# Attention and two gated layers on one core: VectorE's side work moves behind a pass's first sum

## The chip, the cores and the metric

The kernel runs on one core of a Trainium2 chip. The metric is the device time of one execution in microseconds (us). TensorE multiplies matrices into banks of PSUM; VectorE and ScalarE read those banks and do the elementwise work; GpSimd adds one operand per pass; SyncE's queue issues the transfers.

## What is computed

The reference is chunked attention, then two feed-forward layers (cut to what matters):

```python
x = attn_out.transpose(0, 2, 1, 3).reshape(3072, 512)
gate = 1.0 / (1.0 + np.exp(-(x @ w_gate)))      # 512 -> 1536
x = gate * (x @ w_val) @ w_out                  # 1536 -> 512
h = x @ w_in                                    # 512 -> 2048
out = h * (1.0 / (1.0 + np.exp(-h))) @ moe2_w_out   # 2048 -> 512
```

## The kernel before

Every float32 operand is split into a higher part, a rounded copy made on ScalarE (`nc.scalar.copy`, a CAST in the trace), and a lower part, what is left, made on VectorE by a subtraction (`split`, L90 to L99). A product of two operands is three matmuls of the parts: high by high, high by low, low by high.

The tokens stand in blocks. Layer one's first four blocks of 512 tokens are computed plainly, together with the attention of the blocks behind them. Its last 1024 tokens are the "new block" (`b = -1`), computed with seven products of sub-blocks in place of eight; layer two has three such blocks (`b` 0 to 2) of 1024 tokens. The work on one pair of output tiles is a pass (`pair2`): in the new block twelve passes, for six pairs a gate pass ("g") and a value pass ("v"), in a layer-two block eight passes ("l"). Behind the passes `out2` multiplies by the output weights.

A pass is seven products (`prod`) of six matmuls each into three banks: A11 into c1, S1 into c3, S2 into c2, A12 on top of c1, S3 on top of c2, S4 on top of c3, A22 on top of c2. Between two products on the same bank the bank has to be read:
- ScalarE copies c1 behind A11 (`s1`, L1066) and c3 behind S1 (`s5`, L1071); GpSimd adds `s1` to `s5`.
- the first sum `u2 = c2 + s1` is to be done on VectorE (`add`, L998) before S3 may go on with c2;
- the second sum `s5 = c2 + s5` before A22 may go on with c2;
- the third and the fourth sum, behind S4 and A22, bind no product of the same pass.

`done` puts sigmoid or silu (ScalarE) on the sums, `mult` multiplies a value by its gate (VectorE).

Every engine takes its instructions in the order in which the code emits them. Two kinds of side work are emitted among the products. The tail of a pass (`tail_of`): behind the second pass of a pair, the first difference of the output's operands (`sub`, L1001) and the split of the first operand (`form`). And the preparation of the output weights for layer two (`Pace`, `Pair2`): each weight tile is loaded, rebiased on ScalarE (L124), joined on VectorE (L134, L137), four differences are made (L633), the higher parts are cast on ScalarE (`coo`, L761), the lower parts made on VectorE (`lo_of`, L641), and both stored to DRAM (L731). `beat(n)` hands the preparation a time (`PREP2`, per kind of pass), and `Pace.go` emits steps until it is used up; stores are put out two beats behind. In layer one `PREP1` is the time handed out at each of three steps per tile. `prep.finish()` ahead of pass 6 of layer two's first block emits all that is left; then the preparation's pool of memory is closed, and the operands of the last pairs take its place. For `b` 1 and 2 there is no preparation.

Of the kernel before, what the change touches and what calls it, by code (L numbers as in the profile page):

```python
# [8 lines left out]
F32 = mybir.dt.float32  # L9
# [3 lines left out]
ALU = mybir.AluOpType  # L13
# [36 lines left out]
SLOT_C = {i: (n // 4, n % 4) for n, i in enumerate((A11, A12, S1, S2, S3, S4, A22))}  # L50
AHEAD2 = 4
DVE_US = {"meet": 2.1, "norm": 1.75}
PREP1 = 1.95
PREP2 = {"g": (0.4, 0.6, 1.1, 1.1), "v": (0.7, 0.7, 0.3, 0.3), "l": (0.9, 0.9, 1.1, 1.1)}


@with_exitstack
def moe_kernel(ctx: ExitStack, tc: tile.TileContext, qh, kh, vh, wg, wv, wo, w2i, w2o, out):
    nc = tc.nc
# [33 lines left out]
    def split(hi, lo, src, lo_eng, hi_eng=nc.scalar):  # L93

        if hi_eng is nc.scalar:
            nc.scalar.copy(hi, src)  # L96
        else:
            hi_eng.tensor_copy(hi, src)
        lo_eng.tensor_tensor(out=lo, in0=src, in1=hi.bitcast(F32), op=ALU.subtract)  # L99
# [11 lines left out]
    class Unit:  # L111
# [34 lines left out]
        def rest(self):  # L146
            nc.vector.tensor_tensor(
                out=self.u[:, 1], in0=self.t, in1=self.u[:, 0].bitcast(F32), op=ALU.subtract
            )
            if self.keep is not None:  # L150
                nc.sync.dma_start(out=self.keep, in_=self.u.bitcast(F32))
# [235 lines left out]
    with tc.manual_schedule():  # L387
# [169 lines left out]
        src = x32.pop(0)  # L557
# [386 lines left out]
        for b in range(-1, NB2):  # L944
            base[b] = len(granules)
            if b < 0:
# [4 lines left out]
                for i in ORDER2:  # L951
                    for q in range(NPAIRC // 2):
                        if i in (S1, S2, S3, S4):
                            outs.append(wco_d[(S1, S2, S3, S4).index(i), q])
                        else:
                            f, c = 4 * q + (i != A11), 256 * (i == A22)
# [8 lines left out]
        def next_granule():  # L965
            n = loaded[0]
            loaded[0] += 1
            if n >= len(granules):
                return
            w = w_slot(7 + n % NRING, f"wr{n}").rearrange("p a b c -> p (a b c)")  # L970
            k, src, *a = granules[n]
            if k == "o" or k == "m":
                w = w.rearrange("p (b a m c) -> p b a m c", b=2, a=2, m=2)
                if k == "o":
                    nc.sync.dma_start(out=w.bitcast(F32), in_=src)
                else:
                    for j, part in enumerate(src):
                        nc.sync.dma_start(out=w[:, j].bitcast(F32), in_=part)
            else:
                w = w.rearrange("p (a m c) -> p a m c", a=2, m=4)  # L980
                src = wc_d[src[0], src[1]] if k == "c" else w2i_d[src]
                nc.sync.dma_start(
                    out=w[:, :, : a[1]].bitcast(F32), in_=src[:, a[0], :, : a[1]]
                )
            ring[n] = w
# [4 lines left out]
        def bank(name):  # L990
            turn[0] += 1
            return (ps_m, ps_a, ps_m, ps_a, ps_y, ps_y, ps_y, ps_y)[(turn[0] - 1) % 8](name)

        def t2(name):
            return p2.tile([P, 512], F32, tag="t2", name=name, bufs=7)

        def add(o, a, b_):
            nc.vector.tensor_tensor(out=o, in0=a, in1=b_, op=ALU.add)  # L998
# [4 lines left out]
        def silu(o, i):  # L1003
            nc.scalar.activation(out=o, in_=i, func=AF.Silu)  # L1004
# [10 lines left out]
        def pair2(b, p, fill, tail, kind=""):  # L1015

            n = f"{b}_{p}{kind}"
            if kind:
                k = base[b] + 4 * p + 2 * "gv".index(kind)
            else:  # L1020
                k = base[b] + 2 * p
            slot = SLOT_C if kind else SLOT_L2
            final = [max(i, key=ORDER2.index) for i in ([j for j in slot if slot[j][0] == 0], [j for j in slot if slot[j][0]])]
            c1, c2, c3 = bank(f"c1_{n}"), bank(f"c2_{n}"), bank(f"c3_{n}")
            X = xp[b]

            def prod(o, i, first):
                half, m = slot[i]
                w = ring[k + half]
                j = 0  # L1030
                for kt in range(2):
                    for pw, px in ((0, 0), (0, 1), (1, 0)):
                        nc.tensor.matmul(  # L1033
                            o,
                            w[:, pw, m, kt * P : (kt + 1) * P],
                            X[i][:, px, kt],
                            start=first and j == 0,
                            stop=j == 5,
                            skip_group_check=not first,
                        )  # L1040
                        j += 1
                if i in final:
                    next_granule()

            def done(r, c):
                g = g2_of(b, p, r)
                if kind == "g":
                    nc.scalar.activation(out=g, in_=c, func=AF.Sigmoid)
                elif kind == "v":
                    wait.append((g, c))  # L1050
                else:
                    silu(g, c)

            def mult():
                while wait:
                    g, c = wait.pop(0)
                    nc.vector.tensor_tensor(out=g, in0=c, in1=g, op=ALU.mult)

            def beat(n):
                if b < 0 or b == 0 and p < NPAIR - 2:  # L1060
                    prep.go(PREP2[kind if kind else "l"][n] if p or kind == "v" or b == 0 else 0.0)

            wait = []
            s1, s5, u2 = t2(f"s1_{n}"), t2(f"s5_{n}"), t2(f"u2_{n}")
            prod(c1, A11, True)
            nc.scalar.copy(s1, c1)  # L1066
            if tail:
                tail()
            beat(0)
            prod(c3, S1, True)  # L1070
            nc.scalar.copy(s5, c3)  # L1071
            nc.gpsimd.tensor_tensor(out=s5, in0=s5, in1=s1, op=ALU.add)  # L1072
            if fill:
                fill()
            beat(1)
            prod(c2, S2, True)
            add(u2, c2, s1)
            prod(c1, A12, False)
            done("11", c1)
            prod(c2, S3, False)  # L1080
            add(s5, c2, s5)
            mult()
            done("22", s5)
            beat(2)
            prod(c3, S4, False)
            add(u2, c3, u2)
            mult()
            done("12", u2)
            prod(c2, A22, False)
            add(s1, c2, s1)  # L1090
            done("21", s1)
            mult()
            beat(3)

            def tail_of():
                pp = p // 2
                if p % 2 and kind != "g":

                    t = g2[b, pp, "12"]
                    sub(t, t, g2[b, pp, "11"])  # L1100
                    form(b, pp)

            return tail_of

# [12 lines left out]
                o, x, y = {S2: ("12", "22", "12"), S3: ("11", "12", "11"), A22: ("21", "21", "12")}[i]  # L1117
                sub(g2[b, pp, o], g2[b, pp, x], g2[b, pp, y])

        def form(b, m):  # L1120

            form_sum(b, m + 1)
            npp = npp_of(b)
            if m >= 7 * npp:
                return
            i, pp = ORDER2[m // npp], m % npp
            r = {A11: "11", S1: "12", S2: "12", A12: "21", S3: "11", S4: "22", A22: "21"}[i]
            src = g2[b, pp, r]
            f = p2.tile([P, 2, 2, 512], F32R, tag="gf", name=f"gf{b}_{m}", bufs=AHEAD2)
            split(f[:, 0], f[:, 1], src, nc.vector)  # L1130
            gf[b, m] = f

        def out2(b, beside):

# [83 lines left out]
        for bi, n in enumerate(BLOCKS1[:NB1]):  # L1218
# [3 lines left out]
            for f in range(NF1):  # L1222
                it = 3 * (bi * NF1 + f)

                def steps(i):
# [3 lines left out]
                    else:  # L1229
                        prep.go(PREP1 - sum(DVE_US.get(w, 0) for w, t in events.get(it + i, [])))  # L1230
                    if xgen is not None and (it + i) % 3 != 1:
# [53 lines left out]
        for b in range(-1, NB2):  # L1285
            tail = None
            if b < 0:
                for p in range(NPAIRC):
                    for kind in "gv":
                        fill = (lambda: emit_out1(*pending, t2)) if p + "gv".index(kind) == 0 else None  # L1290
                        tail = pair2(b, p, fill, tail, kind)
            else:
                for p in range(NPAIR):
                    if b == 0 and p == NPAIR - 2:
                        prep.finish()
                        pp_cm.__exit__(None, None, None)
                        p3_cm = tc.tile_pool(name="p3", bufs=1, side="right")
                        p3 = p3_cm.__enter__()
                    tail = pair2(b, p, None, tail)
            tail()  # L1300
            if b < 0:
                form(b, NPAIRC // 2)

            def beside(m):
                nonlocal xgen
                if b + 1 == NB2:
                    return
                if m == 0:
                    xgen = x_parts(b + 1, *load_y(b + 1))
                if m in ((4, 5, 6, 10, 11, 12, 17, 18, 19) if b < 0 else (4, 9, 10, 11, 16, 17, 24, 25, 26)):  # L1310
                    next(xgen, None)

            out2(b, beside)
# [76 lines left out]
```

## Time and profile before

| | |
|---|---|
| median of 3 runs | 1121.18 us (1121.1 to 1122.63) |
| profiled execution | 1124.1 us |
| its span | 1122.1 us, 2.0 us of the time lie around it |
| mean granted TensorE clock | 0.992 |
| TensorE, VectorE, ScalarE busy | 97%, 69%, 48% of the span |

The span runs from the first to the last instruction. The granted clock is a share of 2.4 GHz. A busy share is a mean over stages with different limits, and a wait on TensorE shows in the list of waits only if it leaves the engine idle; a slow clock does not show there.

### The profile page before, as it was taken

The page shows a single profiled execution, that of the slowest core. Times are in us where ns is not written, and L with a number is a line of the kernel's source. Part 1 is how long each engine was busy: PE and PEld are TensorE (multiplying, and loading weights), DVE is VectorE, ACT ScalarE, POOL GpSimd, SP SyncE. Part 2 cuts the span into 40 slices and gives each one's busy share as a digit, 9 for nine tenths or more (in the row PEclk, how much of TensorE's full clock was granted, in tenths as well). Part 3 has the DMA queues.
Part 4 walks back from the last instruction along what each step waited for, and adds up shares of the span by engine and source line. Part 5 has one row for each costly group of instructions (what it writes and reads, how often), then busy time and mean ns, then how long its engine had stood idle before and what let it go on. Part 6 is the DMA issues. An engine that isn't in the chain of part 4 may idle for free. (4 is left out here: it accounts for less than half of the span.)

```text
span 1122.1 us, 18930 instructions
## 1 busy us (share of the span) xinstructions
PE 1093.2 (97%) x7580; PEld 893.7 (80%) x7580; DVE 776.6 (69%) x1156; ACT 533.1 (48%) x791; POOL 65.6 (6%) x50
## 2 busy tenths in 40 slices
PE   7999999999999999999999998999999999999998
PEld 4888888888887788877778876788888888888887
DVE  7988787777777777567669857567833479443665
ACT  6766554364444453433434554354434455344442
POOL 0000000000000000011111001101011110011000
PEclk9999999999999999999999998999999999999999
DMA  8788688789877887687888697774755766655561
GB/s 317 274 282 298 230 299 298 274 294 316 310 256 266 288 323 260 227 284 262 295 293 329 196 337 256 271 301 169 251 195 192 269 231 228 207 197 206 195 217 76
DMA packets 106247, 288.02 MB, mean 257 GB/s; under 512 B 8624, under 2 KB 39344, under 8 KB 95408
## 3 DMA queue, kind: packets, MB, share of 16 engines
q1 hardware_dynamic: 105872, 286.43, 72.8%
q8 instruction: 60, 0.98, 0.4%
q10 hardware_dynamic: 288, 0.39, 0.1%
q14 instruction: 27, 0.22, 0.1%
HBM read 210.24 MB, written 76.55 MB: 256 GB/s over the span
## 5 line engine op out<-in xcount | busy, mean ns | idle before, releaser
L1033 PE MATMUL c<-xp,wr 128*128 128x512 f32 x1008 | 235.9, 397 | 8.4 <-DVE u L998 8.4
L1033 PEld LDWEIGHTS c<-xp,wr 128*128 128x128 f32 x1008 | 193.2, 192 | 50.6 <-DVE u L998 9.6
L1182 PE MATMUL o<-gf,wr 128*128 128x512 f32 x1008 | 229.0, 389 | 0.0
L1182 PEld LDWEIGHTS o<-gf,wr 128*128 128x128 f32 x1008 | 189.2, 188 | 39.3
L359 PE MATMUL pv<-x,w 128*128 128x512 f32 x564 | 138.5, 394 | 0.1
L359 PE MATMUL pg<-x,w 128*128 128x512 f32 x564 | 138.4, 394 | 0.1
L99 DVE TENSOR_TENSOR gf<-g,gf 128x1024 fp32r<-128x1024 f32 x84 | 103.9, 1239 | 49.7 <-ACT gf L96 49.2
L96 ACT CAST gf<-g 128x1024 fp32r<-128x1024 f32 x84 | 88.1, 1052 | 86.8 <-PE o L1182 71.5
L359 PEld LDWEIGHTS pv<-x,w 128*128 128x128 f32 x564 | 104.2, 188 | 23.2 <-DVE sg L374 0.4
L359 PEld LDWEIGHTS pg<-x,w 128*128 128x128 f32 x564 | 104.4, 188 | 22.1 <-DVE x L99 0.7
L376 ACT CAST g<-sg 128x512 fp32r<-128x512 f32 x48 | 29.8, 621 | 129.8 <-DVE sg L374 129.7
L998 DVE TENSOR_TENSOR s<-c,s 128x512 f32<-128x512 f32 x48 | 33.2, 691 | 66.3 <-PE c L1033 63.5
L1004 ACT ACTIVATE g<-s 128x512 f32<-128x512 f32 x48 | 30.3, 632 | 62.5 <-DVE s L998 62.5
L1001 DVE TENSOR_TENSOR g<-g,g 128x1024 f32<-128x1024 f32 x48 | 58.4, 1216 | 0.0
L1072 POOL TENSOR_TENSOR s<-s,s 128x512 f32<-128x512 f32 x24 | 35.4, 1476 | 335.7 <-ACT s L1071 335.7
L379 DVE TENSOR_TENSOR g<-sg,g 128x512 fp32r<-128x512 f32 x48 | 33.2, 691 | 26.1 <-ACT g L376 26.1
L998 DVE TENSOR_TENSOR u<-c,s 128x512 f32<-128x512 f32 x24 | 16.5, 688 | 40.2 <-PE c L1033 38.4
L369 ACT ACTIVATE sg<-pg 128x512 f32<-128x512 f32 x48 | 28.6, 596 | 31.2 <-PE pg L359 22.8
L108 PE MATMUL y<-g,wor 128*128 128x512 f32 x144 | 38.6, 390 | 0.0
L104 PE MATMUL y<-g,wor 128*128 128x512 f32 x144 | 38.5, 389 | 0.0
L106 PE MATMUL y<-g,wor 128*128 128x512 f32 x144 | 38.5, 389 | 0.0
L317 DVE STREAM_TRANSPOSE x<-sx 128x512 f32<-128x512 f32 x20 | 14.3, 716 | 33.8 <-PE sx L220 30.3
(596 smaller groups left out, 1574.0 us busy)
## 6 DMA issues: line engine op xcount, KB each, us to landing
wr<-w2o_d SPq DMA_DIRECT2D x42, 1024.0 KB, 4.8
wr<-w2i_d SPq DMA_DIRECT2D x24, 1024.0 KB, 5.5
wor<-wo_d SPq DMA_DIRECT2D x36, 512.0 KB, 7.1
wr<-w2i_d SPq DMA_DIRECT2D x24, 768.0 KB, 4.4
w2o_d<-coo SPq DMA_DIRECT2D x56, 256.0 KB, 6.9
w2i_d<-coi SPq DMA_DIRECT2D x24, 512.0 KB, 7.3
wr<-wc_d SPq DMA_DIRECT2D x12, 1024.0 KB, 6.3
v<-in_vh_dram SPq DMA_DIRECT2D x21, 512.0 KB, 5.6
```

The costliest lines, as they stand in the source:

```text
L96: nc.scalar.copy(hi, src)
L99: lo_eng.tensor_tensor(out=lo, in0=src, in1=hi.bitcast(F32), op=ALU.subtract)
L104: nc.tensor.matmul(o, w_hi, x_hi, start=first, stop=False)
L106: nc.tensor.matmul(o, w_hi, x_lo, start=False, stop=False)
L108: nc.tensor.matmul(o, w_lo, x_hi, start=False, stop=last)
L359: nc.tensor.matmul(o[:, :n], w[:, pw, kt * P : (kt + 1) * P], x[kt][:, px, :n], start=i == 0, stop=i == len(steps) - 1,)
L379: nc.vector.tensor_tensor(out=g[:, 1, :n], in0=sg[:, :n], in1=g[:, 0, :n].bitcast(F32), op=ALU.subtract)
L998: nc.vector.tensor_tensor(out=o, in0=a, in1=b_, op=ALU.add)
L1001: nc.vector.tensor_tensor(out=o, in0=a, in1=b_, op=ALU.subtract)
L1033: nc.tensor.matmul(o, w[:, pw, m, kt * P : (kt + 1) * P], X[i][:, px, kt], start=first and j == 0, stop=j == 5, skip_group_check=not first,)
L1072: nc.gpsimd.tensor_tensor(out=s5, in0=s5, in1=s1, op=ALU.add)
L1182: nc.tensor.matmul(c[at[i], dp], w[:, pw, pl, dp * P : (dp + 1) * P], f[:, px, pl], start=i in (A11, S1, S2) and pp == 0 and j == 0, stop= ...
```

## The change

In `pair2` the tail and the first beat, which stood behind the copy `s1`, are emitted behind the first sum, for the new block and layer two's first block; for `b` 1 and 2 the tail stays where it was. The beat behind S1 is gone, so a pass has three beats, with new times. `form` can return the lower part of its split as a function, which the pass calls behind the second sum. `PREP1` falls from 1.95 to 1.88.

```diff
-PREP1 = 1.95
-PREP2 = {"g": (0.4, 0.6, 1.1, 1.1), "v": (0.7, 0.7, 0.3, 0.3), "l": (0.9, 0.9, 1.1, 1.1)}
+PREP1 = 1.88
+PREP2 = {"g": (0.9, 1.5, 1.3), "v": (0.9, 0.7, 0.2), "l": (1.0, 1.8, 1.6)}
...
-            wait = []
+            wait, early = [], b > 0
             s1, s5, u2 = t2(f"s1_{n}"), t2(f"s5_{n}"), t2(f"u2_{n}")
+            rest = None
             prod(c1, A11, True)
             nc.scalar.copy(s1, c1)
-            if tail:
-                tail()
-            beat(0)
+            if tail and early:
+                tail()()
             prod(c3, S1, True)
             nc.scalar.copy(s5, c3)
             nc.gpsimd.tensor_tensor(out=s5, in0=s5, in1=s1, op=ALU.add)
             if fill:
                 fill()
-            beat(1)
             prod(c2, S2, True)
             add(u2, c2, s1)
+            if tail and not early:
+                rest = tail()
+            beat(0)
             prod(c1, A12, False)
             done("11", c1)
             prod(c2, S3, False)
             add(s5, c2, s5)
+            if rest:
+                rest()
             mult()
             done("22", s5)
-            beat(2)
+            beat(1)
...
-            split(f[:, 0], f[:, 1], src, nc.vector)
+            nc.scalar.copy(f[:, 0], src)
             gf[b, m] = f
+
+            def low():
+                nc.vector.tensor_tensor(
+                    out=f[:, 1], in0=src, in1=f[:, 0].bitcast(F32), op=ALU.subtract
+                )
+
+            if later:
+                return low
+            low()
```

On VectorE, at the start of pass 2 of layer two's first block (names `u_0_2`: block 0, pass 2; `u` is the first sum, `s` the second, `coo` lower parts, `gf` the lower split, `g` the difference), the order before was:

```order
L1001 TENSOR_TENSOR g_0_12_6892<-g_0_12_6892,g_0_11_6865 128x1024
L99 TENSOR_TENSOR gf_0_7009<-g_0_11_6865,gf_0_7009 128x1024
L641 TENSOR_TENSOR coo_0_6991<-fo_6927,coo_0_6991 128x512
L641 TENSOR_TENSOR coo_1_6993<-fo_6927,coo_1_6993 128x512
L641 TENSOR_TENSOR coo_2_7012<-fo_6927,coo_2_7012 128x512
L641 TENSOR_TENSOR coo_3_7015<-fo_6927,coo_3_7015 128x256
L998 TENSOR_TENSOR u_0_2_7000<-c_0_2_6996,s_0_2_6998 128x512
L998 TENSOR_TENSOR s_0_2_6999<-c_0_2_6996,s_0_2_6999 128x512
```

and is now, up to the third sum:

```order
L998 TENSOR_TENSOR u_0_2_7000<-c_0_2_6996,s_0_2_6998 128x512
L1001 TENSOR_TENSOR g_0_12_6897<-g_0_12_6897,g_0_11_6871 128x1024
L641 TENSOR_TENSOR coo_0_6973<-fo_6912,coo_0_6973 128x512
L641 TENSOR_TENSOR coo_1_6993<-fo_6912,coo_1_6993 128x512
L641 TENSOR_TENSOR coo_2_7026<-fo_6912,coo_2_7026 128x512
L641 TENSOR_TENSOR coo_3_7029<-fo_6912,coo_3_7029 128x256
L998 TENSOR_TENSOR s_0_2_6999<-c_0_2_6996,s_0_2_6999 128x512
L1139 TENSOR_TENSOR gf_0_7024<-g_0_11_6871,gf_0_7024 128x1024
L134 TENSOR_SCALAR stg_w2o_6952<-stg_w2o_6952 128x512
L137 SCALAR_TENSOR_TENSOR fo_7056<-stg_w2o_6952 128x2x256
L134 TENSOR_SCALAR stg_w2o_6954<-stg_w2o_6954 128x512
L137 SCALAR_TENSOR_TENSOR fo_7056<-stg_w2o_6954 128x512
```

The difference and the four lower parts moved from ahead of the first sum to between the first and the second, the lower split behind the second, ahead of two joins.

On ScalarE, from the end of pass 4 to the start of pass 6 of the same block (`s` copies of c1 and c3, `g` silu), the order before was:

```order
L761 CAST coo_0_7260<-fo_7205 128x512
L761 CAST coo_1_7262<-fo_7205 128x512
L1066 COPY s_0_5_7267<-c_0_5_7264 128x512
L761 CAST coo_2_7277<-fo_7205 128x512
L761 CAST coo_3_7280<-fo_7205 128x256
L1071 COPY s_0_5_7268<-c_0_5_7266 128x512
L1004 ACTIVATE g_2_11_7223<-c_0_5_7264 128x512
L1004 ACTIVATE g_2_22_7234<-s_0_5_7268 128x512
L1004 ACTIVATE g_2_12_7247<-u_0_5_7269 128x512
L1004 ACTIVATE g_2_21_7258<-s_0_5_7267 128x512
L1066 COPY s_0_6_7349<-c_0_6_7346 128x512
```

and is now:

```order
L1067 COPY s_0_5_7263<-c_0_5_7260 128x512
L1071 COPY s_0_5_7264<-c_0_5_7262 128x512
L1004 ACTIVATE g_2_11_7210<-c_0_5_7260 128x512
L1004 ACTIVATE g_2_22_7222<-s_0_5_7264 128x512
L1004 ACTIVATE g_2_12_7236<-u_0_5_7265 128x512
L1004 ACTIVATE g_2_21_7247<-s_0_5_7263 128x512
L761 CAST coo_0_7323<-fo_7224 128x512
L761 CAST coo_1_7325<-fo_7224 128x512
L761 CAST coo_2_7327<-fo_7224 128x512
L761 CAST coo_3_7330<-fo_7224 128x256
L1067 COPY s_0_6_7349<-c_0_6_7346 128x512
```

The last four casts moved from the start of pass 5 to its end, between its last silu and the first copy of pass 6.

On SyncE's queue the last stores (`w2o_d<-coo`) and the loads of weights (`wr`) stood, around the end of pass 5:

```order
L982 DMA wr_7312<-w2i_d 128x2x768
L731 DMA w2o_d<-coo_0_7260 128x2x256 x2
L731 DMA w2o_d<-coo_1_7262 128x2x256 x2
L975 DMA wr_7335<-w2o_d 128x2048
L731 DMA w2o_d<-coo_2_7277 128x2x256 x2
L731 DMA w2o_d<-coo_3_7280 128x2x256
```

and stand now:

```order
L982 DMA wr_7301<-w2i_d 128x2x768
L975 DMA wr_7319<-w2o_d 128x2048
L731 DMA w2o_d<-coo_0_7323 128x2x256 x2
L731 DMA w2o_d<-coo_1_7325 128x2x256 x2
L731 DMA w2o_d<-coo_2_7327 128x2x256 x2
L731 DMA w2o_d<-coo_3_7330 128x2x256
```

All seven stores stand behind the load that TensorE's last product of pass 5 releases.

## Rows read from the trace of the kernel before

**Rows 1.** The page, busy time of the engines.
```profile
PE 1093.2 (97%) x7580; PEld 893.7 (80%) x7580; DVE 776.6 (69%) x1156; ACT 533.1 (48%) x791; POOL 65.6 (6%) x50
```

**Rows 2.** The waits of TensorE: us in total, times, longest.
```profile
PE c L1033 <- DVE u L998: 8.4, 3, 3.5
...
PE c_-1_2g L1033 <- DVE u_-1_2g L998: 2.5, 1, 2.5
PE c_-1_4g L1033 <- DVE u_-1_4g L998: 2.4, 1, 2.4
...
PE c_-1_4v L1033 <- DVE u_-1_4v L998: 0.9, 1, 0.9
PE c_-1_0v L1033 <- DVE u_-1_0v L998: 0.8, 1, 0.8
```

**Rows 3.** The timeline of TensorE: start us, us, line, idle time before.
```profile
462.21 1.52 PE L1033 MATMUL c_-1_0g<-xp-1_0_5222,wr 128*128 128x512 f32 x6
...
537.13 1.52 PE L1033 MATMUL c_-1_3v<-xp-1_0_5222,wr 128*128 128x512 f32 x6
...
545.29 1.52 PE L1033 MATMUL c_-1_3v<-xp-1_5_5430,wr 128*128 128x512 f32 x6
...
550.73 1.52 PE L1033 MATMUL c_-1_4g<-xp-1_4_5389,wr 128*128 128x512 f32 x6
...
558.86 1.52 PE L1033 MATMUL c_-1_4v<-xp-1_0_5222,wr 128*128 128x512 f32 x6
...
588.61 1.52 PE L1182 MATMUL o_-1_0_6418<-gf-1_0_5788,wr 128*128 128x512 f32 x6
...
645.82 15.12 PE L1033 MATMUL c<-xp,wr 128*128 128x512 f32 x66
```

**Rows 4.** Windows: us, TensorE busy, granted clock, DMA share, GB/s.
```profile
514.00:516.00 2.00, 2.00 (x7) 0.50 1.00 403
...
556.00:558.00 2.00, 2.00 (x11) 1.00 0.96 353
...
680.00:682.00 2.00, 2.00 (x7) 0.50 0.18 11
```

**Rows 5.** The chain that ended last: start us, us, what.
```profile
813.60 76.16 PE c L1033 x336
```

**Rows 6.** The timeline of VectorE.
```profile
495.49 2.32 DVE L641 TENSOR_TENSOR coo<-fo,coo 128x512 fp32r<-128x512 f32 x4
...
507.10 1.22 DVE L1001 TENSOR_TENSOR g-1_0_12_5533<-g-1_0_12_5533,g-1_0_11_5515 128x1024 f32<-128x1024 f32 x1
508.23 2.31 DVE L99 TENSOR_TENSOR gf-1_0_5788<-g-1_0_11_5515,gf-1_0_5788 128x1024 fp32r<-128x1024 f32 x1
...
511.52 0.68 DVE L998 TENSOR_TENSOR u_-1_2g<-c_-1_2g,s_-1_2g 128x512 f32<-128x512 f32 x1
...
544.20 0.69 DVE L998 TENSOR_TENSOR s_-1_3v<-c_-1_3v,s_-1_3v 128x512 f32<-128x512 f32 x1 [2.03 <-PE c_-1_3v L1033]
...
559.67 0.42 DVE L134 TENSOR_SCALAR stg_w2o<-stg_w2o 128x512 int32<-128x512 int32 x1
...
562.06 2.65 DVE L633 TENSOR_TENSOR fo<-fo 128x256 f32<-128x256 f32 x4
...
721.39 1.23 DVE L99 TENSOR_TENSOR gf<-g,gf 128x1024 fp32r<-128x1024 f32 x1 [1.16 <-ACT gf L96]
```

**Rows 7.** The timeline of ScalarE in passes 6 and 7 of layer two's first block.
```profile
729.03 0.60 ACT L1004 ACTIVATE g<-c 128x512 f32<-128x512 f32 x1 [7.18 <-DMA w2o_d<-coo]
...
731.09 0.58 ACT L1066 COPY s<-c 128x512 f32<-128x512 f32 x1
```

**Rows 8.** The timeline of SyncE's queue, the last stores.
```profile
719.96 1.97 SPq L731 DMA_DIRECT2D w2o_d<-coo  x3
```

**Rows 9.** The line of the stores, L731, 56 of them.
```profile
DMA to landing us min/median/max: 4.8/6.9/8.2
```

**Rows 10.** The timeline of TensorE in layer one.
```profile
367.73 0.86 PE L308 MATMUL sx<-v,at 64*32 64x64 f32 x64 [2.33 <-ACT at L293]
```

More of the change, by code (lines that the diff above doesn't have):

```diff
@@ L1092, in pair2 @@
             mult()
-            beat(3)
+            beat(2)
             def tail_of():
@@ L1100, in tail_of @@
                     sub(t, t, g2[b, pp, "11"])
-                    form(b, pp)
+                    return form(b, pp, True)
+                return lambda: None
             return tail_of
@@ L1118, in form_sum, with form @@
                 sub(g2[b, pp, o], g2[b, pp, x], g2[b, pp, y])
-        def form(b, m):
+        def form(b, m, later=False):
             form_sum(b, m + 1)
@@ L1299, in moe_kernel @@
                     tail = pair2(b, p, None, tail)
-            tail()
+            tail()()
             if b < 0:
```

## The prediction

> **What bounds the kernel now.** The head of the profile's page comes first: TensorE is busy for 97% of the span, so only its waits and its slow stretches can be won; VectorE is busy for 69% [rows 1]. The list of what TensorE waited for comes next [rows 2]. One reason stands out: the products' line L1033 waits for a `u` made by VectorE at L998, in three waits of layer two's first block (8.4 us, the longest 3.5) and in four of the new block (2.5, 2.4, 0.9 and 0.8), 15.0 us in all. That `u` is the first sum of a pass, which reads bank c2 before the product S3 may add to it.
>
> A wait costs more than its length. From 537.13 to 545.29 stand six products, so one takes 1.36 us and a pass of seven 9.52 [rows 3]. From 550.73 to 558.86 four products took 8.13 us instead of 5.44: the 2.40 us wait in them cost 2.69, that is 0.29 for starting again, and the granted clock stayed at 1.00 behind it. Behind others it stood at 0.50 (1.2 GHz): behind the 2.45 us wait of the new block and the 3.5 us one of layer two [rows 4].
>
> The loss by stage: from 462.21 to 588.61 stand 516 matmuls (twelve passes of 42, twelve of layer one's). At the pace of a block without waits (336 in 76.16 us [rows 5]) they need 117.0 us and took 126.4: 9.4 lost. Layer two's first block began at 645.82 and ended, one such 76.16 before 813.60, at 737.44: 91.6 us for the same work, 15.3 lost besides the last matmul's own length [rows 3, 5]. Together 24.7 us. Of these 15.0 are the waits, 2.0 seven restarts at 0.29; the 7.7 left are slow clock. With four slow stretches, which I count in the windows, that is 1.9 us for one.
>
> **The change part by part.** T is the start of a pass on TensorE. In a pass without waits (537.13) the second sum starts at T+7.07, and A22, which needs it, at T+8.16 [rows 3, 6]. The first sum starts as long behind its product as the second (0.27), so at T+4.35, and must end before S3 at T+5.44.
>
> *Work moved from ahead of the first sum to behind it.* In the old order the subtraction, the lower split (2.31 us at 508.23) and a join stand ahead of it: the queue is busy from 507.10 to 511.52, where the sum starts without idle time; it ends at 512.2, and S3 had waited 2.45 us for it [rows 2, 6]. In the new order no beat and no tail of the pass itself stands there in any of the eighteen passes with such work, and what the pass before leaves there ends by T+4.6 where I added it up. All seven waits go: -24.7 us.
>
> *What now stands between the first and the second sum.* VectorE starts an instruction some 0.08 before the one ahead ends (508.23 behind the 1.22 us at 507.10), so a sum of 0.69 takes 0.61 of the queue, and there is room from T+4.96 to 8.16 - 0.69 - 0.04, T+7.43: 2.47 us. In most passes what stands there fits (the subtraction's 1.13 with one join, half of the 2.39 from 559.67 to 562.06). In passes 2 and 4 of layer two's first block it doesn't: the subtraction and all four lower parts (2.32, 2.25 to the next start) make 3.38 us [rows 6]. The second sum starts at T+8.34, 0.91 late, and with the restart costs 1.2, twice: +2.4. The low end is the bare 0.9 each, the high end a slow stretch more each.
>
> *What follows behind the second sum.* In those passes the lower split (1.23), two joins (2.39) and the third and fourth sum end at T+13.8; ScalarE's last silu (0.6) follows, and behind it in ScalarE's queue the next pass's copy of c1 (0.58 [rows 7]), which A12 waits for. It ends near T+15.0, where A12 is due at T+14.5 (its pass starts at 9.52 + 0.91): 0.5 late, with the restart 0.8, twice: +1.5. In the new block the gate passes of pairs 2 and 3 leave two casts between that silu and the copy, by the same sum 0.4 and 0.2 late: with restarts +1.2. The low end of these four is nothing, since a few tenths decide.
>
> In the value pass of pair 2 GpSimd's addition, late with that copy, meets VectorE's lower parts. Beside GpSimd a lower split took 2.31 us, and 1.23 elsewhere [rows 6], so 1.08 more; the second sum is then some 0.15 past its room, which I leave inside the range. The Trainium skill, "SBUF — State Buffer", section "SBUF: two separate sides", says that VectorE and GpSimd take a shared pair of ports as an exclusive lock, so that the later one waits for the whole of the other. The row agrees in kind; by the Trainium skill's rule, with GpSimd's whole addition in the way, the same place would cost about 0.3 instead of 0.15 us.
>
> *The last stores.* What is left of the preparation is finished at once behind pass 5: four casts, four lower parts and seven stores together, where before two lower parts and four stores went ahead during pass 5. The silu of pass 6 waits in ScalarE's queue for the last store, as its output lies in memory that the stores' pool gives back: 7.18 us, until 729.03 [rows 7]. Pass 6 began two passes before 737.44, at 718.40, so this is T+10.6; three more silus follow, and pass 7's copy of c1 starts at 731.09 and ends at T+13.27, where A12 needs it at T+13.56: 0.3 us to spare, so it shows as no wait. Now the casts can start only behind pass 5's last silu, at T+1.3, the last lower part (0.65 each) ends at T+4.4, and the stores, at 0.66 us each (three in 1.97), are issued up to T+6.6 instead of T+3.5 [rows 8]. With the median landing of 6.9 us [rows 9] the last lands near T+13.2; ScalarE goes on at T+13.4, the copy ends at T+16.1, 2.6 us late. Landings of 4.8 to 8.2 make this 0.5 to 3.9. Of the six waits of 2 us and over (the sixth is layer one's, at 1.00), four were followed by a slow stretch, so I take one: 2.6 + 0.3 + 1.9 = +4.8.
>
> *Layer one.* The smaller number for its beats shifts the preparation among the forward steps. Its one long wait, 2.33 us at 367.73, is for a copy behind a late gate product [rows 10]; in the new order two joins less stand ahead of the splits at that block's start, which should bring all behind them forward by 2.4 us. Another wait may open elsewhere, as the order changes over the whole layer. I take -1.0, with -2.6 and +2.4 as the ends.
>
> **The sum.** -24.7 + 2.4 + 1.5 + 1.2 + 4.8 - 1.0 = -15.8 us. The profiled execution's 1124.1 becomes 1108.3; the median, 2.9 below it at 1121.2, becomes 1105. A measurement of this kernel can tell about 0.2%, 2.2 us.
>
> **The rivals.** First, *the waits simply go*: the new waits stay at their low ends (0.9 twice, 0.5) and layer one gives its 2.6: -24.7 + 2.3 - 2.6 = -25, 1096 us. For it: all new waits but the two of 0.91 lie within a few tenths of their limits or hang on a landing time. Against it: those two are plain sums of rows. Chance 0.13.
>
> Second, *the waits move*: every larger new wait is followed by a slow stretch and the stores land late. Passes 2 and 4 cost 6.2, the last stores 6.1, the small ones 2.7, layer one 2.4: -24.7 + 17.4 = -7, 1114 us. For it: the 0.50 behind waits as short as 2.45 [rows 4]. Against it: all seven short and long waits of before made only four such stretches. Chance 0.10.
>
> Third, *slower*: the second sum becomes what the first was. Its room is 2.47 us in each of eighteen passes; if VectorE reaches it late in all of them, by 1.1 us and a restart on the mean, the 24.7 us are given back, and from there it is slower: 1124 us and more. For it: the same work must be done in the same passes. Against it: by the order sixteen of the eighteen have less than 2.47 us there, so that nearly every one would have to be stretched by an us, as 2.31 for 1.23 was, and VectorE has a third of the span free [rows 1]. Chance 0.03.
>
> Fourth, *no change*: the first sum isn't late for its queue but for its own input. The wait list names it seven times, and at 511.52 it starts with no idle time ahead of it [rows 2, 6]. Chance 0.02.
>
> **How the numbers follow.** The forecast has 0.72 and ends at about 1098 and 1111. The first rival lies around 1096; a range from 1097 to 1111 takes in a part of it and leaves out about 0.07 below and 0.13 above. Faster by over 0.2% is all but the last two rivals, 0.95; the same 0.02, slower 0.03.
>
> **What would show it.** In the list of waits L1033 no longer waits for the first sum, and waits about 0.9 us for the second sum in passes 2 and 4 of layer two's first block, some tenths for ScalarE's copy L1067 in the passes behind, and 2 to 3 us for that copy in the last pass, behind a silu that the last store releases. The windows show 1.00 everywhere but there. The forecast is wrong if the clock falls behind waits under one us, if the last stores land within 5 us, or if layer one shows a new wait.

## The result and the profile after

| | before | after |
|---|---|---|
| median, its runs | 1121.91 us (1121.1 to 1123.99, 4) | 1107.91 us (1106.93 to 1109.23, 4) |
| ratio | | 0.9873, interval 0.9855 to 0.9891 |
| profiled execution, its span | 1124.1, 1122.1 | 1109.23, 1107.1 |
| mean granted clock | 0.992 | 0.998 |

The kernel is faster by 1.27%, 14.0 us; 1105 was forecast, with 1097 to 1111 around it. The profiled executions differ by 14.9 us.

The list of TensorE's waits after, which answers to [rows 2]:

```profile
PE sx L220 <- issue: 1.7, 1, 1.7
PE c L1033 <- DVE s L998: 1.4, 2, 0.8
...
PE c L1033 <- ACT s L1067: 1.3, 1, 1.3
PE c_-1_5v L1033 <- DVE u_-1_5v L998: 1.2, 1, 1.2
...
PE pv L359 <- DVE sg L374: 0.8, 1, 0.8
PE c_-1_0g L1033 <- DMA wr<-wc_d: 0.6, 1, 0.6
```

The `u` of layer two's first block, 8.4 us before, is gone, and so are those of passes 2g, 4g, 4v and 0v of the new block. Three kinds stand in its place: 1.4 us for the second sum `s` in two passes, 1.3 for ScalarE's copy in one, and 1.2 for a first sum that had been in time, that of the value pass of pair 5 (5v). Layer one shows new waits too: the pause of 1.7 us that stands first in the list, 0.8 for `sg` and 0.6 for the first weights `wr`.

The timeline of TensorE after, which answers to [rows 3], shows the stages:

```profile
386.50 0.32 PE L220 MATMUL sx<-k,q 64*32 64x64 f32 x9 [1.75 <-issue]
386.75 4.61 PE L359 MATMUL pv<-x,w 128*128 128x512 f32 x12
...
465.11 1.63 PE L1033 MATMUL c_-1_0g<-xp-1_0_5194,wr 128*128 128x512 f32 x6 [0.56 <-DMA wr<-wc_d]
...
580.57 1.65 PE L1033 MATMUL c_-1_5v<-xp-1_3_5371,wr 128*128 128x512 f32 x6 [1.25 <-DVE u_-1_5v L998]
...
584.80 1.52 PE L1196 MATMUL o_-1_0_6425<-gf-1_0_5803,wr 128*128 128x512 f32 x6
...
641.92 8.32 PE L1033 MATMUL c<-xp,wr 128*128 128x512 f32 x36
...
716.76 5.73 PE L1033 MATMUL c<-xp,wr 128*128 128x512 f32 x24 [1.27 <-ACT s L1067]
722.33 1.98 PE L1196 MATMUL o<-gf,wr 128*128 128x512 f32 x8
```

The new block's passes take 119.7 us (465.11 to 584.80) where they took 126.4; at full pace they need 117.0. Layer two's first block takes 80.4 (641.92 to 722.33) where, first start to first start, it took 91.5; at full pace 76.2. So the passes gave back 17.8 us, and 7.0 of loss is left in them. But the new block starts at 465.11, not at 462.21 [rows 3]: layer one lost 2.9. The rest of the kernel is the same to 0.1 us.

The windows of TensorE after (us, busy, granted clock, DMA share, GB/s), which answer to [rows 4]:

```profile
388.00:390.00 2.00, 2.00 (x6) 0.50 1.06 413
580.00:582.00 2.00, 1.43 (x6) 1.00 1.06 406
670.00:672.00 2.00, 1.94 (x8) 1.00 0.80 312
718.00:720.00 2.00, 2.00 (x10) 1.00 0.07 29
```

No wait of the passes is followed by a slow stretch (a time at a granted clock of 0.50, 1.2 GHz) any more. The only one of the execution stands in layer one, behind the pause of 1.75 us at 386.50, for which the profile names no releaser.

### The profile page after: what moved, and what is told of

Same layout as the page of the kernel before. It is cut to its first block, busy times and chain, and to the rows that moved or that the text cites. A ratio compares the mean times of both kernels' runs of the same rounds, so it can differ in the third digit from the quotient of the medians.

```text
span 1107.1 us, 18923 instructions
## 1 busy us (share of the span) xinstructions
PE 1087.8 (98%) x7580; PEld 889.8 (80%) x7580; DVE 771.4 (70%) x1156; ACT 532.5 (48%) x791; POOL 64.2 (6%) x50
## 4 chain that ended last, share of the span: by engine, by line
PE 85%; DVE 7%; ACT 3%; DMA 3%; issue 1%; SPq 0%; DVEq 0%; ACTq 0%
PE o L1196 21%; PE c L1033 18%; PE pv L359 10%; PE pg L359 9%; PE y L108 3%; PE y L104 3%; PE y L106 3%; PE sx L308 1%; PE sx L220 1%; PE o_-1_1_6430 L1196 1%; PE o_-1_0_6429 L1196 1%; PE c_-1_0g L1033 1%; PE c_-1_4v L1033 1%; PE c_-1_5g L1033 1%; PE c_-1_1v L1033 1%
## 5 line engine op out<-in xcount | busy, mean ns | idle before, releaser
L1033 PE MATMUL c<-xp,wr 128*128 128x512 f32 x1008 | 230.5, 390 | 2.7 <-DVE s L998 1.4
L1033 PEld LDWEIGHTS c<-xp,wr 128*128 128x128 f32 x1008 | 188.8, 188 | 43.9 <-ACT s L1067 2.5
```

The source lines that it names most:

```text
L1033: nc.tensor.matmul(o, w[:, pw, m, kt * P : (kt + 1) * P], X[i][:, px, kt], start=first and j == 0, stop=j == 5, skip_group_check=not first,)
```

## The experiments

Each ratio is to the kernel before on the same chip, over as many runs as are given. Two medians of the changed kernel differ by 1.2 us (1107.91 above, 1106.68 below), so differences of about a microsecond are read from traces, not from times. `e7_staircase` ran once and has no interval.

| kernel | median us (runs) | ratio, interval |
|---|---|---|
| `e1_prep1_old` | 1107.34 (4) | 0.9855, 0.9842 to 0.9869 |
| `e2_prep1_alone` | 1122.78 (11) | 0.9993, 0.998 to 1.0005 |
| `e3_tail_ahead` | 1107.18 (4) | 0.986, 0.9844 to 0.9875 |
| `e5_tail_alone` | 1108.67 (4) | 0.9874, 0.986 to 0.9887 |
| `e4_low_at_once` | 1109.64 (4) | 0.9882, 0.9869 to 0.9896 |
| `e6_silu_later` | 1105.88 (5) | 0.9842, 0.9829 to 0.9856 |
| `e8_joined` | 1105.43 (4) | 0.9841, 0.9828 to 0.9855 |
| `e9_no_addition` | 1106.41 (4) | 0.9849, 0.9835 to 0.9862 |
| `after_again` | 1106.68 (4) | 0.9859, 0.9843 to 0.9876 |
| `e10_both_sums` | 1105.57 (5) | 0.9844, 0.983 to 0.9859 |
| `e7_staircase` | 1157.92 (1) | |

**Which part gives the gain.** Layer one's number alone, on the kernel before, and its old value in the kernel after:

```diff
-PREP1 = 1.95
+PREP1 = 1.88
```

> The kernel before with 1.88 in place of 1.95 and nothing else. If the number costs by itself, by delaying layer one's preparation, the time is 0.5 to 3 us above before's 1121.9, with the waits at the end of layer one that the changed kernel shows. If it helps by itself (the rival: a shorter wait at 367.73), it is under 1120.

> The changed kernel with layer one's number back at 1.95. If the gain lies in the passes alone (my reading of the two traces), layer one is again as before: the new block starts near 462.2 us instead of 465.1, its waits for a gate product (0.79) and for the first weights (0.56) are gone, the passes stay as they are, and the time is 1105 to 1107, 1 to 3 us under the changed kernel. If the smaller number is part of the gain, the time is 1109 or more.

Neither changes the time by what can be told; with the old value the new block starts at 462.20, as expected. In the list of waits the 1.88 does what was forecast, the 2.33 us wait of [rows 10] goes; but smaller ones open (0.8 for `sg`, 0.4 to 0.9 for the first `wr`), so little is left. It also trades one risk for another: the 2.3 us wait was followed by a slow stretch in three of the five profiles with 1.95, and the pause near 386 us stands in five of the eight with 1.88. The new block starts at 463.2 on the mean of the five and at 463.4 on that of the eight.

Then the two moves apart. In the first kernel the whole tail stands ahead again, behind the copy `s1`, and only the beats are as changed; in the second, whose edit is not shown here, only the tail is moved, and the four beats with their old times, and the 1.95, stand where they were.

```diff
-            wait, early = [], b > 0
+            wait, early = [], True
```

> The changed kernel with the tail (subtraction and whole split) back behind the copy s1 in all blocks, the beats where the change put them. If the tail by itself holds the first sum, five passes show a wait for the first sum of 0.5 to 1.5 us (with the split stretched beside GpSimd), the two waits for the second sum (0.78, 0.65) go, and the time is 1110 to 1113. If only the beats' work held the first sum (the rival), the time is 1105.5 to 1108.

> The kernel before with only the tail moved behind the first sum and its lower split behind the second; four beats at their old places, with the old times and 1.95. By my sums the waits that had a tail ahead (2.45, 2.40, 3.54, 2.79) shrink to under 0.5 us, those that had only beats ahead (0.75, 0.90, 2.03) stay and cost about 6 with the slow stretch, and there are no new ones behind: 1104 to 1108. If the beats carry half of the gain or more (the rival), 1112 to 1117.

Either alone gives nearly the whole gain. The waits of the kernel with the tail ahead:

```profile
PE c L1033 <- DVE u L998: 1.7, 2, 1.4
...
PE c_-1_2g L1033 <- DVE u_-1_2g L998: 1.4, 1, 1.4
...
PE c L1033 <- DVE s L998: 0.5, 2, 0.2
```

and of the one with the tail alone moved:

```profile
PE c L1033 <- DVE u L998: 2.5, 3, 2.0
...
PE c_-1_4v L1033 <- DVE u_-1_4v L998: 0.9, 1, 0.9
PE c_-1_0v L1033 <- DVE u_-1_0v L998: 0.7, 1, 0.7
```

The old loss was an overflow of the queue ahead of the first sum; taking out either the tail or the beats leaves waits of 2 us at most. What the other move saves in addition is mostly lost again further on: TensorE's waits in the passes come to 5.1 us with the tail ahead (4.0 of them for first sums), to 4.3 with the tail alone moved (all for first sums), and to 3.9 with both (1.2 for a first sum, 1.4 for the second sums, 1.3 for pass 7's copy). So the gains of the two don't add. The theory of the first run held in kind and not in size: three new waits for a first sum opened, not five, its passes take only 1.2 to 1.6 us longer than the changed kernel's, and the time is the rival's. The second run's waits came as expected; its median is 0.7 above its range.

**The room between the two sums.** First the lower split at its old place within the tail, then added work in steps.

```diff
-                rest = tail()
+                tail()()
```

> The changed kernel with the lower part of the tail's split emitted at once, between the first and the second sum, instead of behind the second. Theory (the room of 2.47 us between the two sums binds; a split takes 1.14 us of VectorE's queue): the second sum comes 1.14 us later wherever a tail stands. From the changed kernel's trace: gate pass of pair 2, second sum starts 513.19 + 1.14, 0.86 late; gate pass of pair 4 has 0.56 of idle time ahead of it, 0.2 late; passes 2 and 4 of layer two's first block wait 0.78 and 0.65 now, so 1.92 and 1.79; pass 6 about 0.45. With a restart of 0.29 for each new wait the sum is 0.86 + 0.2 + 2.28 + 0.45 + 0.9 = +4.7 us against the changed kernel, 1111 to 1113 us, up to 1116 if two slow stretches follow. Rival (the place of the lower split is hidden, or what is lost here is won back at the next first sum): within 1.5 us of the changed kernel, no wait for a second sum over 1 us.

The timeline of TensorE in layer two's first block of this kernel:

```profile
670.81 20.95 PE L1033 MATMUL c<-xp,wr 128*128 128x512 f32 x84 [1.91 <-DVE s L998]
693.54 19.38 PE L1033 MATMUL c<-xp,wr 128*128 128x512 f32 x84 [1.78 <-DVE s L998]
713.23 5.73 PE L1033 MATMUL c<-xp,wr 128*128 128x512 f32 x24 [0.31 <-DVE s L998]
719.64 5.74 PE L1033 MATMUL c<-xp,wr 128*128 128x512 f32 x24 [0.68 <-ACT s L1067]
```

The waits of passes 2 and 4 are 1.91 and 1.78, where 1.92 and 1.79 were worked out; 2g waits 0.71 (0.86), pass 6 0.31 (0.45), 4g none (0.2). The sums with their restarts take 4.1 us more than in the profiled execution after, where 4.7 was worked out. But 1.7 of that is won back behind them, as most of the copies that had been late are in time and pass 7's is less late by 0.6. The passes take 3.9 us more all the same (120.3 and 83.7 us), as a slow stretch behind the wait of 1.91 adds 1.6 (84 matmuls in 20.95 us, 19.38 behind the 1.78). The median, 1109.64, lies below the range expected: the second sum was late as worked out, but the price left out what the rival had in mind, that a part is won back.

```diff
+            for _ in range(p + 4 * (b - 1) if b > 0 else 0):
+                nc.vector.tensor_tensor(out=u2, in0=u2, in1=u2, op=ALU.max)
             if tail and not early:
```

> The changed kernel with p instructions more on VectorE between the first and the second sum of pass p of layer two's second block, and p + 4 in its third (each the maximum of u2 with itself, 128x512, so that nothing else changes). One takes 0.61 us of the queue, the room is 2.47. Theory: four fit, five make the second sum 0.58 us late, six 1.2, seven 1.8, eight 2.4, nine 3.0, ten 3.6, eleven 4.2; TensorE waits just so long in passes 5 to 7 of the second block and 1 to 7 of the third, 20.4 us in all, and 0.29 more for each of the ten starts. Of the clock: the waits before the change were followed by 1.2 GHz behind four of six of 2 us and over, so two or three of the five waits of 2 us and more should be, and none below 2 us; a rival (any wait can, with the same chance) has some below 1.5 us. Time 1107.9 + 23.3 = 1131 without slow stretches, up to 1141 with five of 1.9.

The timeline of TensorE in layer two's third block of this kernel, one row behind each wait (passes 0 to 7, four to eleven instructions):

```profile
972.46 9.86 PE L1033 MATMUL c<-xp,wr 128*128 128x512 f32 x42 [0.27 <-DVE s L998]
983.31 9.81 PE L1033 MATMUL c<-xp,wr 128*128 128x512 f32 x42 [0.99 <-DVE s L998]
995.14 9.84 PE L1033 MATMUL c<-xp,wr 128*128 128x512 f32 x42 [2.02 <-DVE s L998]
1007.43 11.42 PE L1033 MATMUL c<-xp,wr 128*128 128x512 f32 x42 [2.46 <-DVE s L998]
1022.21 11.40 PE L1033 MATMUL c<-xp,wr 128*128 128x512 f32 x42 [3.36 <-DVE s L998]
1037.52 12.30 PE L1033 MATMUL c<-xp,wr 128*128 128x512 f32 x42 [3.91 <-DVE s L998]
1054.76 12.22 PE L1033 MATMUL c<-xp,wr 128*128 128x512 f32 x42 [4.94 <-DVE s L998]
1072.34 2.93 PE L1033 MATMUL c<-xp,wr 128*128 128x512 f32 x6 [5.37 <-DVE s L998]
```

VectorE in pass 5, nine instructions:

```profile
1029.64 0.69 DVE L998 TENSOR_TENSOR u<-c,s 128x512 f32<-128x512 f32 x1 [3.85 <-PE c L1033]
1030.37 6.50 DVE L1078 TENSOR_TENSOR u<-u 128x512 f32<-128x512 f32 x9
1036.78 0.68 DVE L998 TENSOR_TENSOR s<-c,s 128x512 f32<-128x512 f32 x1
```

TensorE waits 29.5 us in twelve passes, not 20.4 in ten, and the time, 1157.92, is far over the 1131 to 1141 expected. The waits are longer because these instructions take more of the queue: each reads what the one before it wrote and starts after its end, 0.73 us from start to start (as from 1029.64 to 1030.37) instead of 0.61. With this pace the room comes out nearly right. The second sum starts 7.14 us behind the first; by the room of 2.47 it may start 0.61 + 2.47 = 3.08 behind it, so 4.06 late, and TensorE waited 3.91. With five (0.73 x 5 + 0.61 - 3.08 = 1.18) it waited 0.99, with seven (2.64) 2.46. So the room is about 2.6 us. With six, eight and ten the waits lie 0.1 to 0.3 us above this pattern: there the addition on GpSimd comes later and the added instructions beside it take 0.2 to 0.35 us longer.

The rows also price the clock: 42 matmuls take 9.8 us behind waits up to 2.02 and 11.4 or 12.3 behind 2.46 and over, so a slow stretch costs 1.6 to 2.5 us. Seven of the twelve waits were followed by one, and none of the five others was longer than 2.02 us, so the rival (any wait, with the same chance) fell. The theory's "none below 2 us" did not hold either: in the same execution the pause of 1.74 us in layer one and a wait of 1.95 us for pass 7's copy were each followed by one.

**The copy of pass 7.** The silus of pass 6 are emitted behind pass 7's two copies, with the changed kernel's 1.88, and then with 1.95.

```diff
+                elif b == 0 and p == NPAIR - 2:
+                    held.append((g, c))
                 else:
                     silu(g, c)
...
+            if p == NPAIR - 1:
+                while held:
+                    silu(*held.pop(0))
             if fill:
```

> The changed kernel with the four silus of pass 6 of layer two's first block emitted behind the two copies of pass 7, so that the copies no longer stand behind the silu that waits for the last store. Theory (the copy of pass 7 is late only because of that silu): the wait of 1.27 us for the copy L1067 in pass 7 goes and nothing takes its place: -1.3 to -1.6 us, about 1106.3. Rival (the silus are themselves needed in time: behind the copies they push pass 7's own silus and the difference behind them back): a wait of 1 us or more appears at the start of the output products, no change within 0.5 us.

> The silus of pass 6 behind pass 7's copies as in the run of that name, and 1.95 for layer one's number in place of 1.88. Theory (the two pieces touch different stages): the gains add up, -0.6 (as 1107.34 to 1107.91 before) and -1.4, about 1105.9, the fastest of the kernels so far. Rival (1.95 and 1.88 differ by chance alone): the same as the run with the silus moved, about 1106.5.

The wait for `s L1067` is in neither list of waits, and nothing takes its place: layer two's first block takes 78.8 and 78.7 us. The medians are 1105.88 and 1105.43; the second is the fastest of all kernels here, but the intervals don't part the two from each other, nor clearly from the kernel after. The rival of the first, a later wait at the output products, fell; that of the second, that 1.95 and 1.88 differ by chance, stands.

**GpSimd's addition.** It is left out of the passes, so the sums with `s5` lack `s1`.

```diff
-            nc.gpsimd.tensor_tensor(out=s5, in0=s5, in1=s1, op=ALU.add)
```

> The changed kernel without GpSimd's addition of s1 to s5 in the passes (the sums with s5 then lack s1: this part of the computation is left out). Theory (VectorE is held up while GpSimd adds): in the value pass of pair 5 a difference took 1.51 us instead of 0.42 beside the addition, and the first sum came 1.25 us late behind it; without the addition 0.15 of that is left. The stretched difference of pass 2 (1.36 for 1.22) gives 0.14 more. Every VectorE instruction of one form then has one duration. About -1.5 us with the restart, 1106.4. Rival (the first sum of that pass is late for the joins behind a late rebias, GpSimd or not): that wait stays at 1 us or more and the time within 0.5 us of the changed kernel.

VectorE in pass 5v of the kernel after, and GpSimd's addition beside it:

```profile
575.40 0.69 DVE L137 SCALAR_TENSOR_TENSOR fo<-stg_w2o 128x512 int32<-128x512 int32 x1 [0.46 <-ACT g-1_2_21_6172 L1048]
...
577.27 2.65 DVE L633 TENSOR_TENSOR fo<-fo 128x256 f32<-128x256 f32 x4
579.83 0.68 DVE L998 TENSOR_TENSOR u_-1_5v<-c_-1_5v,s_-1_5v 128x512 f32<-128x512 f32 x1
```

```profile
577.30 1.53 POOL L1072 TENSOR_TENSOR s_-1_5v<-s_-1_5v 128x512 f32<-128x512 f32 x1 [8.18 <-DVE fo L137]
```

and VectorE in the same pass without the addition:

```profile
573.55 1.55 DVE L633 TENSOR_TENSOR fo<-fo 128x256 f32<-128x256 f32 x4
575.02 0.68 DVE L998 TENSOR_TENSOR u_-1_5v<-c_-1_5v,s_-1_5v 128x512 f32<-128x512 f32 x1
```

The four differences take 1.55 instead of 2.65 us, and the wait of 5v is gone; the new block's passes take 118.0 us (461.94 to 579.98), 1.65 less. The theory held, but the gain didn't stay. The chain of this kernel, with TensorE in pass 7:

```profile
704.00 6.45 DMA w2o_d<-coo
713.31 7.36 PE c L1033 x24
```

Here the last store took 6.45 us to land, the copy came 1.81 us late, and a slow stretch followed (24 matmuls in 7.36 us, 5.73 after). A copy in pass 6 was 0.69 late too. Layer two's first block took 83.4 us, 3.0 more. That the median is the 1106.4 expected is therefore in part chance.

The same holding-up stood in the kernel before, where the prediction did not count it among the causes of the old loss. Ahead of each of the seven late first sums one instruction of VectorE is 1.0 to 1.1 us longer than elsewhere, beside GpSimd's addition. In pass 0v of the kernel before it is a join (0.69 elsewhere):

```profile
478.31 1.29 POOL L1072 TENSOR_TENSOR s_-1_0v<-s_-1_0v 128x512 f32<-128x512 f32 x1 [8.00 <-DVE stg_w2o L134]
```

```profile
478.37 1.78 DVE L137 SCALAR_TENSOR_TENSOR fo<-stg_w2o 128x512 int32<-128x512 int32 x1
```

VectorE has work without a break from there to the sum, so about 7.0 of the 15.0 us of waits are this, and the waits of 0v and 4v (0.75 and 0.90) are nothing else. In the kernel after it still adds 4.2 us in six passes, but makes only 5v's first sum late, as the side work held up stands behind that sum or has room there. No run leaves the addition out in the old order, so what that alone would give is not shown.

**Once more, and one step further.**

> The changed kernel once more, beside the two below. Two things are asked of its profile: whether the pause of 1.75 us at 386.50 in layer one, with no releaser, is there again (theory: it belongs to this order of layer one, as three of the five profiles with 1.88 beside it show 1.4 to 1.5 us there and none of the four with 1.95 does; rival: chance, gone in this one), and how late pass 7's copy is (theory: 0.6 to 1.3 us, as it hangs on the landing of the last stores; rival: 1.27 again, as it hangs on the order alone). Median 1107 to 1109.

The chain of this second profile of the changed kernel:

```profile
706.30 4.17 DMA w2o_d<-coo
713.34 5.74 PE c L1033 x24
```

Its waits in the passes are the same to 0.01 us (0.78, 0.65, 1.25) but for pass 7's copy, 0.97 us late here: that one hangs on the landing, not on the order alone. The pause at 386 us isn't there, so the order doesn't fix it, and the new block starts at 462.04. Over all profiles the pause (1.4 to 1.75 us) stands in five of the eight executions with 1.88 and in none of the five with 1.95. The median, 1106.68, is a little under the range expected.

```diff
-                rest = tail()
+                rest = (lambda: tail()()) if b == 0 else tail()
...
-                elif b == 0 and p == NPAIR - 2:
+                elif b == 0 and (p == NPAIR - 2 or p < NPAIR - 2 and r in ("12", "21")):
...
-            if p == NPAIR - 1:
+            if b == 0 and not kind:
```

> The joined kernel (silus of pass 6 behind pass 7's copies, 1.95) with two more moves in layer two's first block: the whole tail stands behind the second sum, and the silus of each pass's third and fourth sum stand behind the next pass's two copies in ScalarE's queue. Theory (passes 2 and 4 lose only the lateness of the second sum, and work pushed behind it may grow once the copies no longer stand behind the silus): the two waits of 0.65 us go, with their restarts -1.9 us: about 1103.5. Rival (VectorE is full in these passes: 2.2 + 4.5 us of side work and 2.4 of sums in 9.5): the lateness goes on to the next pass's first or second sum, a wait of 0.5 us or more there, no gain.

The rival held. The waits of this kernel:

```profile
PE c L1034 <- DVE u L998: 2.8, 2, 1.4
```

The second sum is in time, and the next pass's first sum is 1.4 us late instead, twice. The queue of VectorE in these passes has no gap left (from the first sum at 663.72 to the end of the next pass's at 675.86 it is idle for 0.1 us at a time at most), so work can only be moved from one wait to another. But it is not all work: 0.9 and 1.0 of the two 1.4 us are a difference that stands beside GpSimd's addition (1.33 and 1.44 us, 0.42 elsewhere).

## Why the prediction was right, and where its sizes were off

**First sums, -24.7.** All seven waits went, and with them all four slow stretches. But the step that what the pass before leaves there "ends by T+4.6" failed in one of the eighteen passes: in 5v a join waited 0.46 us for ScalarE, and the differences behind it were stretched by 1.10 us beside GpSimd's addition. That cost 1.5 us with its restart. The prediction priced the contention of the two engines in pair 2's value pass only. There it came as priced (a lower part took 1.06 us longer, 1.08 forecast) and made no wait; the place in 5v was missed, and without the addition that wait goes. VectorE was held as long as the addition had left: the addition ended at 578.83, and in this trace the difference that started at 577.61 ended at 579.12, 0.29 behind it, where alone it takes 0.42. By the Trainium skill, "SBUF — State Buffer", section "SBUF: two separate sides", the later engine waits for the whole of the other. These rows agree with it: what is added is the rest of the other's time, next to nothing at its end, and not the flat 1.08 us that the prediction took from one row.

**Second sums, +2.4.** Right in place and nearly in size: 0.78 and 0.65 instead of 0.91 and 0.91, 2.0 us with what follows. The added work shows that the room is some 0.15 larger than the 2.47 worked out.

**Copies, +1.5 and +1.2.** In the right passes but smaller: in passes 3 and 5 the copy was just late enough for 0.5 us together, in 2v and 3v for 0.8, with restarts. VectorE's rows of pass 2 show why. The lower split, both joins and the sums run from 669.33 to 674.61, T+13.65 where T+13.8 was forecast, and the last of ScalarE's queue follows by 0.6 and 0.57: a tenth and a half decides between late and in time.

**The last stores, +4.8.** In the passes this is the term with the largest error: it came to 1.6 us. ScalarE after, which answers to [rows 7]:

```profile
703.16 1.96 ACT L761 CAST coo<-fo 128x512 fp32r<-128x512 f32 x4
...
714.08 0.60 ACT L1004 ACTIVATE g<-c 128x512 f32<-128x512 f32 x1 [7.04 <-DMA w2o_d<-coo]
...
716.13 0.57 ACT L1067 COPY s<-c 128x512 f32<-128x512 f32 x1
```

The mechanism was right: the four casts stand together behind pass 5, the silu waits for the last store, and the copy comes late. Wrong was the step with "the median landing of 6.9 us": the lower parts were done at T+4.3 as forecast (T is 701.70), but the stores followed each other 0.4 to 1.8 us apart and not 0.66, so that the last was issued at 710.00, T+8.3 and not T+6.6; and it landed only 3.90 us later. The seven landed from 709.79 to 713.90, one each 0.68 us, while they were issued over 5.5 us. So here the stream sets the last landing: the first store's landing (5.3 us after its issue at 704.52) and six intervals. A median over 56 stores is no price for the last of a burst. The slow stretch didn't come, as the wait was 1.27 and not 2.6 us; where the first landing came later (6.8 us, without the addition), lateness and slow stretch did come.

**Layer one, -1.0.** The long wait went as forecast, but this execution lost 2.9 us: the pause of 1.75 us and the slow stretch behind it (`pv` at 386.75 takes 4.61 us, in the second profile 3.01) are 3.4 of it. Without the pause, in the second profile, layer one is 0.2 us ahead of before. So the term is about 0, and 2.9 on the profiled execution, outside the ends given for it. The cause of the pause is open; no run here tells why some executions with 1.88 have it.

**The sum.** The measured terms give -24.7 + 1.5 + 2.0 + 1.3 + 1.6 + 2.9 = -15.4 against the -14.9 measured, with 0.5 not assigned. The forecast of -15.8 comes so near because layer one's error (3.9 too good) covered those of the stores and the copies (3.2 and 1.4 too bad): that part is luck. Of the prediction's own three signs of being wrong two came: the last stores landed within 5 us, and layer one shows new waits. The mechanism held in the passes, with the sizes above; layer one was wrong. In the median, 1107.91 for 1105, the error is larger, as 2.9 us were taken off for the distance of before's profiled execution from a median of three; here that distance is 1.3, and the nine to fifteen runs of before beside the later kernels have medians of 1123.2. Beside nine of them the changed kernel's second measurement is 16.5 us faster.

One reading was off: pass 6 of the kernel before begins at 718.21 and not at 718.40, so its copy in pass 7 had 0.1 us to spare and not 0.3.

**The rivals.** "The waits simply go" fails at the second sums; "the waits move" fails at its slow stretches, as none of the new waits in the passes is longer than 1.3 us. The third one's room was the right thing to measure: when added work fills it, TensorE waits for every 0.73 us beyond it. The fourth, that the first sum waits for its own input, fell with the seven waits.

## What to carry to other kernels

Two edits that empty the same queue ahead of the same deadline don't add: the first takes the overflow away and the second moves work to the next deadline, so price them as alternatives. Work out the room between two deadlines from rows and count what stands in it, and where the engine is full over the whole pass, moving can only choose which wait shows. Before work is moved, compare the length of each instruction ahead of the deadline with its length elsewhere: here about half of the old lateness was time in which GpSimd held VectorE up. The seven stores issued together here landed at the pace of the stream, so price the last of a burst from the first one's landing and the interval, not from a median.

## What the runs showed of the hardware

- TensorE's clock behind a wait, from 30 us of each execution on: in the rows of these runs waits up to 1.47 us were never followed by 1.2 GHz, those of 2.46 us and over always. Between them it is open in each execution: of 20 waits of 1.74 to 2.45 us twelve were (1.74, 1.75 and 1.81 among them), eight were not (1.78, 2.02 and 2.40 among them). The 2.45 us wait of the new block was in the profile of before and was not in that of 1.88 alone. In the first 30 us, where TensorE waits often, two of the thirteen executions (`e5_tail_alone`, `e10_both_sums`) show 1.2 GHz from about 20 us on, behind waits of 1.7 and 1.17 us.
- VectorE beside GpSimd: an instruction with both operands in SBUF that starts during GpSimd's addition ends later by what was left of the addition less 0.13 to 0.15 us, in all 147 such cases of the thirteen profiles: 1.74 for 0.68 us (start 0.10 into the 1.30 us addition at 520.41), 1.88 for 1.22 (0.51 into that at 706.15), 1.35 for 1.22 (1.04 into that at 664.87). The sums, which read a bank of PSUM, are not held: 345 of them start during an addition, and each takes the usual 0.69 us to 0.01.
- Seven stores of 256 KB issued together (one each 0.4 to 1.8 us) land 0.60 to 0.81 us apart, most of them 0.67 to 0.70, in the ten executions with the beats moved; one interval of these sixty is 1.19. Where four are issued and then three, as in the kernel before, the intervals are 0.2 to 3.7 us.
- VectorE instructions of 128x512 that work in place, each on the result of the one before, follow at 0.73 us from start to start; others at 0.61 (`e7_staircase`).
